# Chunkwise retention with its matmuls placed between the feed-forward matmuls

## The chip, the cores and the metric

The kernel runs on one core of a Trainium2 chip. The metric is the time of one execution in microseconds (us), measured on the device; a profile of one execution is taken beside it. All runs quoted here were in the fast state (no execution was over 1.5% above the fastest of its kernel), and each was compared with runs of the kernel before on the same chip.

In both kernels TensorE does the matrix products and leaves them in tiles of PSUM (called banks here); VectorE and ScalarE work on tiles element by element; GpSimd and SyncE mostly issue transfers (DMA) from and to the main memory, HBM (125 loads by GpSimd and 36 stores by SyncE on the page before). Before each matmul, TensorE loads one operand into its array (the weight load, PEld in the profiles; 2272 loads and 2272 matmuls on the page after).

## The reference

Causal retention over 8 batches, 8 heads, 576 positions and 64 dimensions, followed by a feed-forward layer with a quick Gelu. Cut to what matters:

```python
scores = (1 / np.sqrt(64)) * np.matmul(q, k.transpose(0, 1, 3, 2))   # q, k, v: (8, 8, 576, 64) fp32
gamma  = 1.0 - 2.0 ** (-5.0 - np.arange(8))
Dmat   = np.where(rel >= 0, gamma[:, None, None] ** rel, 0.0)        # rel = query position - key position
x      = np.matmul(scores * Dmat, v)     # then laid out as (4608 tokens, 512)
h      = x @ w_in                        # (512, 2048)
g      = h / (1.0 + np.exp(-1.702 * h))
out    = g @ w_out                       # (2048, 512), fp32
```

Because the decay is a power of gamma, `gamma ** (i - j)` splits into a factor of the query position and one of the key position. So the sum over old keys can be kept as a running 64 x 64 state per head instead of being computed again for every query.

## The kernel before

Two blocks, one after the other. The attention block works on one batch and two heads at a time (32 groups), with the full lower triangle of 576 x 576 scores. Three engines hand tiles to each other: TensorE makes scores, VectorE and ScalarE scale them, TensorE multiplies by v.

```python
# attention block, TensorE
T(0); T(1); A_w1(0)                 # T: transposes of q and k; A: scores; Bph: times v
for g in range(NG):                 # NG = 32
    if g >= 1: Bph(g - 1)
    A_w2(g)
    if g + 2 < NG: T(g + 2)
    if g + 1 < NG: A_w1(g + 1)
Bph(NG - 1)
...
# feed-forward block, TensorE: 4 matmuls up and 4 down for each of 9 chunks x 16 slices
hT(0); hT(1); hT(2)
for F in range(TOT):
    outmm(F)
    if F + 3 < TOT: hT(F + 3)
...
# feed-forward block: ScalarE makes the sigmoid, VectorE multiplies it in
act.activation(s_sb[F % 2].ap(), psH[F % 3].ap(), AF.Sigmoid, scale=1.702)
dve.tensor_tensor(gT[F % 4].ap(), psH[F % 3].ap(), s_sb[F % 2].ap(), ALU.mult)
...
# at each chunk end, ScalarE empties four banks over three staging tiles
for r in range(4):
    m = 4 * c + r
    if m >= 3:
        act.wait_ge(sem_ODMA[m % 3].sem, 16 * ((m - 3) // 3 + 1))
    act.activation(osb[m % 3].ap(), psOut[r].ap(), AF.Copy)
```

## Time and profile before

| | before |
|---|---|
| measured time | 439.0 us (median of 3) |
| attention block | to 165.6 us |
| feed-forward block, first to last matmul | 165.6 to 432.7 us, 267.1 us |
| 1152 feed-forward matmuls at their pitch of 216 ns | 248.8 us |

A word on pitch. A matmul line of the profile gives a duration, 380 ns for 512 columns, but in the timeline eight 512-column matmuls take 1.73 us, 216 ns each: one starts before the one before it has ended. So what a matmul costs here is the distance from its start to the next start.

The head of the page of the kernel before (busy time of each engine; then tenths of busy time in 40 slices of the span, and the granted TensorE clock in tenths; the lines of PEld, POOL and DMA are left out):

```profile
PE 363.5 (83%) x2600; PEld 177.9 (41%) x2624; DVE 219.3 (50%) x515; ACT 215.7 (49%) x390; POOL 105.5 (24%) x132
PE   0450588888888879998989989989989899899894
DVE  7660288888888883333433433433333343344331
ACT  3760388888888853334343343343433433433433
PEclk9995599999999997999999999999999999999999
```

Slices 1 to 15 are attention. From the sixth on, all three engines stand at 8 tenths nearly throughout, and none at 9: no engine is the limit by itself, they wait for each other. The fourth slice is empty. The table of windows of the same kernel (columns: stretch, its length, busy us and instructions of each engine, granted clock, DMA share, GB/s):

```profile
33.00:44.00 11.00, 0.00 (x0) 0.00 (x0) 0.00 (x0) 0.00 (x0) 2.45 (x3) 0.50 1.78 182
45.00:100.00 55.00, 43.76 (x598) 26.42 (x598) 41.47 (x123) 40.65 (x76) 54.54 (x66) 0.91 3.26 146
200.00:300.00 100.00, 94.26 (x422) 41.98 (x432) 37.35 (x54) 39.06 (x68) 0.00 (x0) 1.00 0.11 39
```

From 33 to 44 us nothing computes: the loads of the second batch stand behind 8 MB of weights (issued from 14.9 us on, the batch's from 18.3; w_out took 23.5 us to land, and TensorE began again at 49.3). From 200 us on, TensorE is busy 94 of 100 us. The missing part is at the chunk ends, as the timeline of one of them shows (start, duration, engine, line, what; in brackets the idle time before it and what ended it; the lines between these three are left out):

```profile
197.60 1.58 ACT L516 ACTIVATE osb<-psOut 128x512 f32<-128x512 f32 x3 [0.27 <-PE psOut L550]
200.33 0.60 ACT L516 ACTIVATE osb<-psOut 128x512 f32<-128x512 f32 x1 [1.16 <-DMA out_dram<-osb]
200.98 0.10 PEld L550 LDWEIGHTS psOut<-w_out_sb,gT 128*128 128x128 bf16 x1 [1.66 <-ACT osb L516]
```

The fourth copy waits 1.16 us for a store to free one of the three staging tiles, and TensorE's next weight load waits for that copy.

One more loss stands at the start of the block: in the window from 166 to 171 us the granted clock is 0.50, and the first 13 feed-forward matmuls start 0.43 us apart, twice 0.216, which costs about 2.7 us.

### The profile page before, as it was taken

What the parts mean: (1) busy time and instruction counts of PE and PEld (TensorE: products, weight loads), DVE (VectorE), ACT (ScalarE), POOL (GpSimd) and SP (SyncE); (2) the same over time, 40 slices, a digit from 0 to 9 for tenths busy, and PEclk for the clock granted to TensorE, in tenths of its full rate; (3) what the DMA queues carried; (4) which work ended last, traced back from release to release, by engine and by line L of the source; (5) the groups of instructions that cost most, each with busy time, mean ns of one, the idle gap of its engine ahead of it and who ended that gap; (6) DMA issues with size and microseconds to landing.
All of it is one profiled execution on the core that took longest, in us unless ns stands there. A gap on an engine that the chain in (4) does not pass through costs nothing.

```text
span 438.9 us, 7043 instructions
## 1 busy us (share of the span) xinstructions
PE 363.5 (83%) x2600; PEld 177.9 (41%) x2624; DVE 219.3 (50%) x515; ACT 215.7 (49%) x390; POOL 105.5 (24%) x132
## 2 busy tenths in 40 slices
PE   0450588888888879998989989989989899899894
PEld 0230355545554543443434434434444344344341
DVE  7660288888888883333433433433333343344331
ACT  3760388888888853334343343343433433433433
POOL 9972899997820000000000000000000000000000
PEclk9995599999999997999999999999999999999999
DMA  9999999999980000002011020020020200200202
GB/s 82 145 206 182 148 146 145 146 146 146 141 58 1 1 1 1 1 0 97 0 58 39 0 96 1 1 98 0 16 81 0 96 1 0 97 1 0 98 0 96
DMA packets 120369, 28.24 MB, mean 64 GB/s; under 512 B 113168, under 2 KB 115216, under 8 KB 120336
## 3 DMA queue, kind: packets, MB, share of 16 engines
q0 software_dynamic: 115152, 18.36, 72.2%
q1 hardware_dynamic: 5184, 9.44, 5.7%
q8 instruction: 21, 0.34, 0.4%
q14 instruction: 12, 0.10, 0.1%
HBM read 36.70 MB, written 9.44 MB: 105 GB/s over the span
## 4 chain that ended last, share of the span: by engine, by line
PE 55%; DMA 4%; ACT 2%; issue 1%
PE psOut L550 27%; PE psH L537 27%; DMA out_dram<-osb 4%; ACT osb L516 2%
## 5 line engine op out<-in xcount | busy, mean ns | idle before, releaser
L586 DVE TENSOR_TENSOR gT<-psH,s_sb 128x512 bf16<-128x512 f32 x144 | 99.6, 692 | 167.6 <-ACT s_sb L572 167.6
L550 PE MATMUL psOut<-w_out_sb,gT 128*128 128x512 bf16 x564 | 150.4, 380 | 12.1 <-ACT osb L516 10.5
L572 ACT ACTIVATE s_sb<-psH 128x512 bf16<-128x512 f32 x144 | 85.9, 597 | 151.4 <-PE psH L537 151.4
L537 PE MATMUL psH<-xT,w_in_sb 128*128 128x512 bf16 x564 | 148.2, 384 | 2.3 <-PEq L127 1.7
L550 PEld LDWEIGHTS psOut<-w_out_sb,gT 128*128 128x128 bf16 x576 | 56.5, 98 | 86.4 <-ACT osb L516 18.6
L537 PEld LDWEIGHTS psH<-xT,w_in_sb 128*128 128x128 bf16 x576 | 56.9, 99 | 69.7 <-issue 2.7
L426 ACT ACTIVATE rett_0<-psS_1,vfac 128x448 bf16<-128x448 f32 x64 | 37.1, 580 | 23.7 <-PE psS_1 L313 21.0
L253 PE MATMUL psTq<-ident,st_q 128*128 128x128 bf16 (+1 forms) x160 | 18.1, 228 | 35.7 <-issue 19.9
L459 DVE TENSOR_TENSOR rett_0<-psS_0,Emb 128x512 bf16<-128x512 f32 x32 | 22.1, 692 | 39.8 <-issue 36.4
L170 POOL DMA_DIRECT2D st_v<-in_v_dram x40 | 34.9, 1000 | 13.4 <-issue 10.8
L426 ACT ACTIVATE rett_1<-psS_1,vfac 128x448 bf16<-128x448 f32 x64 | 36.7, 573 | 0.0
L154 POOL DMA_DIRECT2D st_q<-in_q_dram x40 | 34.6, 975 | 3.5 <-issue 2.0
L161 POOL DMA_DIRECT2D st_k<-in_k_dram x40 | 34.7, 1006 | 0.0
L396 ACT ACTIVATE qT_sb<-psTq 128x576 bf16<-128x576 bf16 x32 | 20.8, 649 | 20.7 <-PE psTq L253 20.7
L253 PEld LDWEIGHTS psTq<-ident,st_q 128*128 128x128 bf16 (+1 forms) x160 | 10.8, 101 | 46.3 <-issue 43.5
L276 PE MATMUL psS_0<-qT_sb,kT_sb 64*128 64x128 bf16 x256 | 19.5, 226 | 10.2 <-DVE rett_0 L492 8.8
L340 PE MATMUL psO<-rett_0,st_v 128*64 128x512 bf16 (+3 forms) x128 | 27.7, 315 | 0.2 <-issue 0.2
L340 PE MATMUL psO<-rett_1,st_v 128*64 128x512 bf16 (+3 forms) x128 | 27.6, 315 | 0.1
L305 PE MATMUL psS_0<-qT_sb,kT_sb 64*64 64x64 bf16 (+2 forms) x192 | 20.0, 219 | 9.0 <-DVE rett_1 L459 8.6
L516 ACT ACTIVATE osb<-psOut 128x512 f32<-128x512 f32 x36 | 19.5, 598 | 14.1 <-DMA out_dram<-osb 9.9
L347 PE MATMUL psO<-rett_0,st_v 128*64 128x64 bf16 (+1 forms) x160 | 25.1, 199 | 0.0
L347 PE MATMUL psO<-rett_1,st_v 128*64 128x64 bf16 (+1 forms) x160 | 24.8, 199 | 0.0
(42 smaller groups left out, 301.4 us busy)
## 6 DMA issues: line engine op xcount, KB each, us to landing
out_dram<-osb SPq DMA_DIRECT2D x36, 256.0 KB, 2.3
st_q<-in_q_dram POOLq DMA_DIRECT2D x32, 128.0 KB, 9.2
st_k<-in_k_dram POOLq DMA_DIRECT2D x32, 128.0 KB, 9.2
st_v<-in_v_dram POOLq DMA_DIRECT2D x32, 128.0 KB, 9.1
w_in_sb<-in_moe_w_in_dram POOLq DMA_DIRECT2D x4, 512.0 KB, 10.7
w_out_sb<-in_moe_w_out_dram POOLq DMA_DIRECT2D x1, 2048.0 KB, 23.5
st_q<-in_q_dram POOLq DMA_DIRECT2D x8, 64.0 KB, 9.7
st_k<-in_k_dram POOLq DMA_DIRECT2D x8, 64.0 KB, 9.6
```

Source lines behind the costliest of these rows:

```text
L154: gp.dma_start(stq[0:rows, j, :, :], qkv_src(q, b, j)).then_inc(sem_q_[sl].sem, 16)
L161: gp.dma_start(stk[0:rows, j, :, :], qkv_src(k, b, j)).then_inc(sem_k_[sl].sem, 16)
L170: gp.dma_start(stv[0:rows, j, :, :], qkv_src(v, b, j)).then_inc(sem_v_[sl].sem, 16)
L253: pe.matmul(outT, lhsT, ident[0:rows, 0:rows], is_transpose=True).then_inc(sem_T.sem, 1)
L340: pe.matmul(o, lhsT, rhs, start=(j == 0), stop=(j == 3), skip_group_check=True,)
L347: mm = pe.matmul(o1, lhsT, rhs1, start=(j == 0), stop=(j == 4), skip_group_check=True,)
L426: act.activation(rett[rb][hh][:, jj, 128 : 128 + shi], psS[hh][1][:, 0:shi], AF.Copy, scale=vfac[:, NJ * head + jj : NJ * head + jj + 1],) ...
L516: act.activation(osb[m % 3].ap(), psOut[r].ap(), AF.Copy).then_inc(sem_OEV.sem, 1)
L537: mm = pe.matmul(psH[t].ap(), lhsT, rhs, start=(cc == 0), stop=(cc == 3))
L550: mm = pe.matmul(psOut[r].ap(), lhsT, rhs, start=(f == 0), stop=(f == NF - 1))
L572: act.activation(s_sb[F % 2].ap(), psH[F % 3].ap(), AF.Sigmoid, scale=1.702).then_inc(sem_sig.sem, 1)
L586: dve.tensor_tensor(gT[F % 4].ap(), psH[F % 3].ap(), s_sb[F % 2].ap(), ALU.mult).then_inc(sem_G.sem, 1)
```

## The change

Three things at once. Attention is done in 36 units of 128 tokens, all eight heads, with the state of old keys accumulating in a PSUM bank. Every matmul of a unit is 128 columns wide or less. And there is one instruction stream: each iteration issues one unit's attention matmuls and then 16 up-projection and 16 down-projection matmuls of earlier chunks (units run 4 ahead of the up-projection and 12 ahead of the down-projection). The quick Gelu is one ScalarE function (597 ns a tile on the page after, as the sigmoid before); VectorE no longer takes part in the feed-forward. A small recorder computes the semaphore waits from what each operation reads and writes.

The diff, cut to the main loop and the operations of a unit (setup, semaphores and the recorder are left out):

```diff
-NJ = 5
-JROWS = [128, 128, 128, 128, 64]
+NU = (B * S) // P          # 36 units
+LAG = 12
...
+        def state(u):       # running state: keys times values, accumulated in psK
+            for hp in range(HP):
+                op("pe", lambda e, hp=hp: e.matmul(
+                    psK[:, hp, :], kn[sl][:, 2 * hp : 2 * hp + 2, :],
+                    vp[u % 3][:, 2 * hp : 2 * hp + 2, :],
+                    start=(c == 0 and hp == 0), stop=True, skip_group_check=True), ...)
...
+        for t in range(-2, NU + LAG):
+            if t + 2 < NU:
+                scale_v(t + 2)                 # VectorE
+            if 0 <= t < NU:
+                state(t)                       # 4 matmuls
+            if t + 2 < NU:
+                transposes(t + 2)              # 8 matmuls, 1 VectorE copy
+            if 0 <= t < NU:
+                state_out(t)                   # VectorE
+                inter(t)                       # 4 matmuls, query times state
+                if t < 4:
+                    load_wout(t)
+                load(t + NLD)
+            if 0 <= t + 1 < NU:
+                scores(t + 1)                  # 8 matmuls on 64-row halves
+                scores_out(t + 1)              # 2 on VectorE
+            if 0 <= t < NU:
+                values(t)                      # 8 matmuls on 64-column halves
+                values_out(t)                  # VectorE
+            ch, hq = divmod(t - 4, 4)
+            co, r = divmod(t - LAG, 4)
...
+            for s in range(4):
+                if 0 <= ch < NCH:
+                    up(ch, 4 * hq + s, nh)     # 4 matmuls, 1 Gelu on ScalarE
+                    nh += 1
+                if 0 <= co < NCH:
+                    down(co, r, s, bank)       # 4 matmuls
+            if 0 <= co < NCH:
+                down_out(co, r, bank)          # 1 copy on ScalarE, 1 store
```

The load queue starts with the first four units, then w_in quarters alternating with units:

```diff
+        load_qk(0)
+        setup()
+        load_v(0)
+        for u in range(1, 4):
+            load(u)
+        for i in range(4):
+            load_win(i)
+            load(4 + i)
```

## The prediction

> **What bounds the kernel now.** It runs two phases in sequence. The table of windows shows TensorE at 19.4 of 20 us in the 180-200 us stretch and 94-95 of 100 us after it: the feed-forward phase (about 165.6 to 434 us) is bound by TensorE. Its steady pace in the timeline is 1.73 us for 8 matmuls of 512 columns, so 216 ns each. 1152 of them need 248.8 us; the phase takes about 268 us because at each of the 9 chunk ends the four output banks are emptied over three staging tiles, and the chain of waits has ScalarE waiting for an output store (up to 1.2 us) and TensorE waiting for ScalarE (up to 1.7 us).
> The first 165 us are attention. There every engine is partly idle: TensorE 43.8 of 55 us "busy" at 45-100 us, but those durations overlap. The timeline shows a 3.85 us period per head pair, a ping-pong of TensorE, VectorE and ScalarE; and no TensorE work at all from 33 to 44 us, where the second batch's loads queue behind 8 MB of weights.
>
> **What changes.** Attention becomes 36 units of 128 tokens, all heads, with a running state, and its matmuls stand between feed-forward matmuls. Attention no longer has its own 165 us; it costs only its TensorE time.
> - TensorE per unit, from start-to-start pitches in the before trace: transposes 8 x 56 ns; state 4 x 56; state times query 4 x 56; scores 8, two at a time on 64-row halves, 56 ns a pair; values 8, two at a time on column halves, 59 ns a pair. Sum 1.36 us. The trace shows 0.07-0.1 us lost at each change between full and half array; three or four changes give about 1.7 us per unit (estimate).
> - VectorE per unit: six tiles of 0.65-0.7 us (128x512 from PSUM: 692 ns before), about 4.2 us; the feed-forward multiply (692 ns x 144) disappears into one ScalarE Gelu. ScalarE per unit: four Gelus and one copy, 5 x 0.60 = 3 us. One full iteration is 32 x 216 ns + 1.7 = 8.6 us, so both are slack; in the 8 iterations without second matmuls it is 5.2 us, still above VectorE's 4.2.
> - DMA: same 36.7 MB read, but in the order needed. [...]
>
> **Sum.** Feed-forward can start when units 0-3 are done and, since TensorE is in order, unit 6's keys and queries have landed. With the before kernel's landed bytes over time (0.9, 2.5, 4.8 MB after 11, 22, 33 us) that is about 31 us. Then 31.5 + 248.8 + 31 units x 1.7 (53) [...] + 1 DMA stalls + 3.3 tail (one copy 0.6, one store about 2) = 340 us.
>
> Predicted 340 us, 8 in 10 within 330-356. Faster by over 2%: 0.98; within 2%: 0.01; slower: 0.01.
>
> **What would show it.** TensorE above 95% busy from about 35 us on; first up-matmul near 31 us; the chain of waits nearly all TensorE; 32 feed-forward matmuls plus attention in 8.6 us in the middle; VectorE about 50%, no ScalarE wait at chunk ends; DMA spread over 300 us.
>
> **What would make it wrong.** The start: units' loads delayed behind input weights (first up-matmul at 40 us). Small matmuls interleaved costing more than their pitch, because weight loads or semaphore waits break the pipeline (2.5 us per unit would add 25 us). VectorE setting the pace in the 8 iterations without second matmuls. Gelu slower than the sigmoid, with two PSUM banks instead of three.

Cut from the text: an allowance for a slow TensorE clock at the start of the feed-forward matmuls, with its term in the sum. The sum on record came to 339.3 us, put as 340; without the cut term of 1.7 us, the terms printed above come to 337.6.

## The result, and the profile after

The changed kernel took 338.58 us (median of 4 runs, 338.12 to 339.27) against 439.31 us. The ratio is 0.7703, with a 95% interval of 0.7676 to 0.7731. Ratios here are the mean time of one kernel's fast runs over that of the other's in the same rounds, so not quite the ratio of the medians quoted beside them. In the batches with the experiments the changed kernel itself, run again, took 339.33 us (0.7699).

The head of the page after, the same lines as before (the clock line is discussed below):

```profile
PE 316.9 (94%) x2272; PEld 162.5 (48%) x2272; DVE 132.6 (39%) x229; ACT 115.4 (34%) x198; POOL 108.5 (32%) x135
PE   1676999999999999999999999999999999999995
DVE  2687766864444434444444434444443200000000
ACT  5400345443333333333333333333333344442211
PEclk9999999999999999999999999999999999999999
```

From the fifth slice on, which begins at 33.7 us, TensorE is at 9 (90% or more) until the last slice. The table of windows says it in us:

```profile
45.00:100.00 55.00, 55.00 (x456) 28.97 (x455) 31.97 (x53) 23.28 (x39) 27.31 (x34) 1.00 1.34 159
100.00:200.00 100.00, 100.00 (x742) 51.90 (x740) 42.91 (x70) 34.63 (x58) 33.12 (x39) 1.00 0.69 95
```

One unit's attention in the middle of the run, TensorE alone, from the timeline (the values, eight lines from 151.43 to 151.63, are left out):

```profile
150.12 0.39 PE L305 MATMUL psK<-vp,kn 128*128 128x128 bf16 x4
150.34 0.39 PE L293 MATMUL psT<-ident,kn 128*128 128x128 bf16 x4
150.56 0.39 PE L293 MATMUL psT<-ident,qn 128*128 128x128 bf16 x4
150.79 0.39 PE L326 MATMUL psO<-qkT,kv_0 128*128 128x128 bf16 x4
151.10 0.40 PE L342 MATMUL psS<-qkT 64*128 64x128 bf16 x8
...
151.78 1.04 PE L374 MATMUL psH<-xT,w_in_sb 128*128 128x512 bf16 x4
```

Four full-array matmuls stand 0.22 us apart, 56 ns each. The eight scores, in pairs on row halves, take no longer than four full ones (0.40 us from the first start to the last end, against 0.39). No line has a bracket: nothing waited. The unit takes 1.66 us; the next unit starts at 158.70, an iteration of 8.58 us.

Adding up TensorE's starts over the whole trace gives the account of the span:

| part of the span | estimated in the prediction | measured, us |
|---|---|---|
| before the first feed-forward matmul | 31.5 | 33.8 |
| feed-forward matmuls, with the half-clock loss at their start | 248.8, and the cut 1.7 | 250.5 |
| attention after that point | 53 | 48.1 |
| waiting for loads after that point | 1 | 0 |
| from the last matmul's start to the end | 3.3 | 4.3 |
| sum | 339.3 | 336.7 |

The half-clock loss is visible in TensorE's weight loads at the start of the feed-forward, but not in the clock figure of the view. First the window, with a granted clock of 1.00 (the figure after the x5), then the loads in it from the timeline:

```profile
33.00:36.00 3.00, 3.00 (x21) 1.30 (x18) 3.00 (x6) 0.28 (x1) 3.00 (x5) 1.00 1.86 208
```

```profile
34.20 0.15 PEld L374 LDWEIGHTS psH<-xT,w_in_sb 128*128 128x128 bf16 x1 [0.28 <-issue]
34.63 0.15 PEld L374 LDWEIGHTS psH<-xT,w_in_sb 128*128 128x128 bf16 x1 [0.28 <-issue]
35.06 0.15 PEld L374 LDWEIGHTS psH<-xT,w_in_sb 128*128 128x128 bf16 x1 [0.28 <-issue]
```

They stand 0.43 us apart, twice the 0.216 of the matmuls later on; four matmuls were that slow, which cost 0.85 us.

The 1.00 is not a record of full clock. The clock events kept in this trace begin at 35.54 us, with full clock, and the view counts time without an event as full (so does the PEclk line above). From 35.48 us on the loads stand 0.22 us apart, so the event and the pitch agree. Where an event covers the slow stretch, the view does say 0.50: from 166 to 171 us in the kernel before, and from 150.8 to 153.1 us in the run `seq` below, whose first feed-forward loads also stand 0.43 us apart.

That the second row of the table matches to the tenth, with the cut term, is luck. The term allowed 1.7 us for a slow clock; 0.85 us was the clock, and another 0.85 us is one wait at 303.9 us, where a matmul starts 1.07 instead of 0.22 us after the one before because its bank has not been copied out.

The measured time of that execution is 338.57 us, 1.9 us more than the span. The prediction took its sum for the measured time, so part of its closeness is errors that cancel.

### The profile page after: what moved, and what is told of

Same layout as the page of the kernel before. It is cut to its first block, busy times and chain, and to the rows that moved or that the text cites. A ratio compares the mean times of both kernels' runs of the same rounds, so it can differ in the third digit from the quotient of the medians.

```text
span 336.7 us, 5221 instructions
## 1 busy us (share of the span) xinstructions
PE 316.9 (94%) x2272; PEld 162.5 (48%) x2272; DVE 132.6 (39%) x229; ACT 115.4 (34%) x198; POOL 108.5 (32%) x135
## 2 busy tenths in 40 slices
DMA packets 87447, 32.85 MB, mean 98 GB/s; under 512 B 76416, under 2 KB 80512, under 8 KB 87424
## 4 chain that ended last, share of the span: by engine, by line
PE 89%; POOL 6%; DMA 3%; ACT 0%; issue 0%; POOLq 0%
PE psH L374 38%; PE psY L392 31%; PE psS L392 4%; PE psT L293 4%; PE psO L359 3%; DMA qn<-in_q_dram 3%; PE psS L342 3%; PE psO L392 2%; POOL kn L200 2%; PE psK L305 2%; POOL vn L214 2%; POOL qn L200 2%; PE psO L326 1%; POOL w_in_sb L223 1%; ACT osb L401 0%; PE psO L332 0%
## 5 line engine op out<-in xcount | busy, mean ns | idle before, releaser
L379 ACT ACTIVATE gT<-psH 128x512 bf16<-128x512 f32 x144 | 86.0, 597 | 182.9 <-PE psH L374 182.9
L392 PE MATMUL psY<-w_out_sb,gT 128*128 128x512 bf16 x480 | 122.2, 379 | 0.7 <-ACT osb L401 0.7
L392 PEld LDWEIGHTS psY<-w_out_sb,gT 128*128 128x128 bf16 x480 | 46.5, 98 | 57.9 <-ACT osb L401 2.4
L296 DVE COPY qkT<-psT 128x1024 bf16<-128x1024 bf16 x36 | 24.8, 690 | 108.0 <-PE psT L293 107.9
L200 POOL DMA_DIRECT2D kn<-in_k_dram x40 | 36.8, 928 | 94.8 <-PE psK L305 80.3
L214 POOL DMA_DIRECT2D vn<-in_v_dram x40 | 37.4, 947 | 2.5 <-issue 2.4
L200 POOL DMA_DIRECT2D qn<-in_q_dram x40 | 37.0, 935 | 0.0
L284 DVE TENSOR_TENSOR vp<-vn,vfac 128x512 bf16<-128x512 f32 x36 | 24.6, 685 | 13.9 <-DMA vn<-in_v_dram 13.9
L350 DVE TENSOR_TENSOR pm_1<-psS,mask 128x512 bf16<-128x512 f32 x32 | 21.8, 680 | 0.0
L350 DVE TENSOR_TENSOR pm_0<-psS,mask 128x512 bf16<-128x512 f32 x32 | 21.8, 680 | 0.0
L359 PE MATMUL psO<-pm_1,vp 128*64 128x128 bf16 x144 | 15.9, 237 | 0.0
L359 PE MATMUL psO<-pm_0,vp 128*64 128x128 bf16 x144 | 15.9, 237 | 0.0
```

Source lines behind the costliest of these rows:

```text
L200: e.dma_start(dst[p0 : p0 + n, :, :], src[b, :, s0 : s0 + n, :].rearrange("h p d -> p h d"),)
L214: e.dma_start(vn[sl][p0 : p0 + n, :, :], v[b, :, s0 : s0 + n, :].rearrange("h p d -> p h d"),)
L284: op("dve", lambda e: e.tensor_tensor(vp[u % 3].ap(), vn[sl].ap(), vfac[:, ty, :, None].to_broadcast([P, H, DH]), ALU.mult), reads=[f"vn{s ...
L296: op("dve", lambda e: e.tensor_copy(qkT[u % 3].ap(), psT.ap()), reads=["psT"], writes=[f"qkT{u % 3}"])
L350: op("dve", lambda e, hh=hh: e.tensor_tensor(pm[u % 2][hh].ap(), psS[hh].ap(), m[:, None, :].to_broadcast([P, HP, P]), ALU.mult), reads=[f ...
L359: op("pe", lambda e, hp=hp, hh=hh: e.matmul(psO[64 * hh : 64 * hh + 64, hp, :], vp[u % 3][:, 2 * hp + hh, :], pm[u % 2][hh][:, hp, :], sta ...
```

## The experiments

Twelve runs were made, one of them the changed kernel again. All gave correct results.

### The yardstick: the changed kernel again

> The changed kernel unaltered, as the yardstick for the runs beside it on the same chip: 338 to 339 us.

339.33 us, ratio 0.7699. The first feed-forward matmul was at 34.0 us here.

### Is it the overlap, or the smaller work? The same units without interleaving

```diff
-        for t in range(-2, NU + LAG):
+        for t in range(-2, NU):
...
                 values(t)
                 values_out(t)
+        for t in range(4, NU + LAG):
             ch, hq = divmod(t - 4, 4)
```

Nine xT tiles (they hold attention's result, the input of the feed-forward) take the place of three, so that all attention can be finished first. The matmuls are the same.

> The changed kernel with the same units and the same matmuls, but no interleaving: all attention units first, then all feed-forward matmuls (nine xT tiles instead of three). Theory (the gain is the overlap; attention alone is bound by loads, VectorE and the chain between engines, not by TensorE): attention phase 36 units x 4.3 to 4.9 us = 155 to 180 us, then 249 us, so 410 to 430 us. Rival (the gain is the smaller work of the chunkwise form, interleaved or not): attention phase of 36 x 1.66 = 60 us plus a start of 10 to 20, total 325 to 345 us.

It took 407.54 us (407.32 to 408.41), ratio 0.9275. The first feed-forward matmul was at 150.8 us. The windows of this kernel show who was busy in the two parts:

```profile
45.00:100.00 55.00, 43.41 (x448) 31.09 (x446) 50.76 (x85) 0.00 (x0) 44.98 (x55) 1.00 1.80 199
200.00:300.00 100.00, 100.00 (x466) 44.07 (x464) 0.00 (x0) 43.43 (x74) 0.00 (x0) 1.00 0.11 40
```

and the chain of waits between 59 and 63 us says what set the pace (start, duration, what):

```profile
59.45 1.20 DVE pm L350 x2
60.65 0.60 DVE xT L368
61.24 0.60 DVE vp L284
61.84 0.60 DVE qkT L296
62.44 0.60 DVE kv L315
63.04 1.20 DVE pm L350 x2
```

It is VectorE without a gap: six tiles of 0.60 us, 3.6 us per unit. That is the pace from 60 us on; before, units came 4.3 to 5.7 us apart from 21 us on, with VectorE and TensorE waiting for loads in between. The theory had said 4.3 to 4.9 us per unit and 410 to 430 us, so the mechanism (loads, then VectorE, not TensorE) holds and its size was too large. The rival (325 to 345 us) falls. Going to the chunkwise form, with the cleaner feed-forward part that comes with it, is worth 32 us of the gain (439.8 to 407.5); letting the two parts share the time is worth the other 68 (407.5 to 339.3; the two kernels ran in different batches, with 439.8 and 440.0 us for the kernel before). The split holds for this order of steps: the old attention was not run interleaved, and what the single Gelu function is worth was not isolated.

### Is TensorE really the limit, and is 56 ns the price? Every transpose twice

```diff
-                for hp in range(HP):
+                for hp in [h for h in range(HP) for _ in range(2)]:
                     op("pe", ... is_transpose=True ...)
```

> Every transpose is issued twice (same input, same place, result unchanged): 8 more matmuls of 128 columns per unit. Theory (TensorE is the only limit once feed-forward has started, and an interleaved small matmul costs its 56 ns pitch and nothing else): 8 x 56 ns = 0.45 us in each of the 30 units that are transposed after the start, so +13.4 us, 352 us. Rival 1 (TensorE has slack in the pipeline, another engine or DMA sets the pace): under +3 us. Rival 2 (interleaved small matmuls cost much more than their pitch): over +20 us.

351.82 us, 12.5 us more than the yardstick. In the trace a unit's attention went from 1.66 to 2.11 us, as its first line and the feed-forward's next show:

```profile
148.26 0.39 PE L305 MATMUL psK<-vp,kn 128*128 128x128 bf16 x4
...
150.37 1.04 PE L374 MATMUL psH<-xT,w_in_sb 128*128 128x512 bf16 x4
```

The difference is 8 x 56 ns; over the 29 units transposed after the start it is 13.0 us. So TensorE had no slack that could have hidden the extra matmuls, and a small matmul among large ones costs its pitch and nothing more. Both rivals fall.

### What does a change of array shape cost?

```diff
+            if 0 <= t + 1 < NU:
+                scores(t + 1, (0, 1))
             if 0 <= t < NU:
                 inter(t)
...
-                scores(t + 1)
+                scores(t + 1, (2, 3))
```

> The score matmuls of a unit (64-row halves) are split in two groups with the state-times-query matmuls (full array) between them; same matmuls, two more changes between full and half array in the 28 units that have a state. Theory (each change of array use costs about 0.1 us beyond the 0.056 us pitch: 0.15 us from start to start in the after trace): 28 x 2 x 0.1 = +5 to +6 us. Rival (the 0.1 us is a wait for a semaphore or VectorE that happens to stand there): 0 to +1 us.

343.99 us, 4.7 us more, just under the expected 5 to 6. A unit with a state took 1.88 us instead of 1.66, for two more changes: 0.11 us each. The expectation counted 28 units with a state; 24 of them stand after the first feed-forward matmul, and there the attention grew from 48.1 to 53.2 us. The timeline of such a unit, where the scores now stand on both sides of the state product:

```profile
153.29 0.39 PE L293 MATMUL psT<-ident,qn 128*128 128x128 bf16 x4
153.61 0.29 PE L342 MATMUL psS<-qkT 64*128 64x128 bf16 x4
153.83 0.40 PE L326 MATMUL psO<-qkT,kv 128*128 128x128 bf16 x4
154.16 0.29 PE L342 MATMUL psS<-qkT 64*128 64x128 bf16 x4
```

The first four transposes of q need 0.22 us, but the scores start 0.32 us after them. That is about 0.1 us lost at the change, and 0.11 us by the unit's total. The changed kernel has three such changes per unit, and about 0.1 us is lost at each in its timeline above: from full array to row halves (scores, 151.10), to column halves (values, 151.43) and back (151.78). What TensorE does in that time the traces do not show.

### Is VectorE slack?

Two more multiplies per unit, into scratch tiles:

```diff
+            for x in range(2):
+                n = (2 * u + x) % 4
+                op("dve", lambda e, n=n: e.tensor_tensor(
+                    junk[n].ap(), vn[sl].ap(),
+                    vfac[:, ty, :, None].to_broadcast([P, H, DH]), ALU.mult), ...)
```

> Two more VectorE multiplies of 128x512 per unit, 0.6 to 0.69 us each, into scratch tiles. Theory (VectorE is slack in the 8.58 us iterations, and close to the pace only in the eight 5.12 us iterations without second matmuls and in the start): VectorE per unit rises from about 4.2 to 5.4 us, +2 to +7 us, all of it before 76 us; middle iterations stay at 8.58 us. Rival (VectorE sets the pace): +1.2 us per unit, over +35 us.

339.61 us, 0.3 us more than the yardstick: slack, even more of it than expected. The windows of this kernel, first in the stretch of the short 5.12 us iterations, then in the middle:

```profile
45.00:74.00 29.00, 29.00 (x273) 15.34 (x271) 27.95 (x47) 13.30 (x23) 19.28 (x24) 1.00 1.88 215
100.00:200.00 100.00, 100.00 (x752) 52.35 (x751) 57.39 (x94) 34.87 (x60) 33.26 (x39) 1.00 0.69 95
```

VectorE is busy 27.95 of 29 us and TensorE still 29.00 of 29. The error in the expectation was to add up busy durations (0.68 us each). Back-to-back tiles start 0.60 us apart, so eight of them need 4.8 us and fit in 5.12. The +2 us lower bound was missed for that reason. Only the start was 1.0 us later (first feed-forward matmul at 35.0 us).

### How much of the gain could the feed-forward part have had alone?

The kernel before with six staging tiles:

```diff
-osb = [sb(f"osb{i}", [P, 512], FP32) for i in range(3)]
+osb = [sb(f"osb{i}", [P, 512], FP32) for i in range(6)]
-                        act.wait_ge(sem_ODMA[m % 3].sem, 16 * ((m - 3) // 3 + 1))
+                        act.wait_ge(sem_ODMA[m % 6].sem, 16 * ((m - 6) // 6 + 1))
```

(and the same modulus at the other places)

> The kernel before with six output staging tiles instead of three: takes away ScalarE's wait for an output store at the chunk ends, nothing else. Theory (of the about 19 us that the feed-forward phase lies above 1152 x 216 ns, the store wait of 1.2 us at each of 8 or 9 chunk ends is half): -8 to -10 us, 430 us. Rival (the store wait is hidden and the four ScalarE copies in a row are the whole stall): 0 to -2 us. Either way it says how little of the 100 us gain can be had in the feed-forward phase.

429.23 us, ratio 0.9764: 10.5 us less, as the theory had it. The feed-forward block shrank from 267.1 to 256.7 us. The timeline of the same chunk end (other lines are left out):

```profile
195.93 2.06 ACT L516 ACTIVATE osb<-psOut 128x512 f32<-128x512 f32 x4 [0.27 <-PE psOut L550]
197.07 0.10 PEld L550 LDWEIGHTS psOut<-w_out_sb,gT 128*128 128x128 bf16 x1 [0.33 <-ACT osb L516]
197.56 0.10 PEld L550 LDWEIGHTS psOut<-w_out_sb,gT 128*128 128x128 bf16 x1 [0.40 <-ACT osb L516]
198.05 0.10 PEld L550 LDWEIGHTS psOut<-w_out_sb,gT 128*128 128x128 bf16 x1 [0.39 <-ACT osb L516]
```

The four copies now follow each other, and TensorE follows the copies. The store wait was about 10 of the 18 us that the block lay above its floor of 248.8. Of the 7.9 us that are left, about 5.9 us are lost where the matmuls follow the four copies (in each of eight chunk ends three of them start 0.40 to 0.49 instead of 0.22 us apart), and about 1.8 us the half clock at the start of the block. The changed kernel empties one bank per iteration, beside other matmuls, and keeps one such wait of 0.85 us.

### The start: what does it wait for?

The first feed-forward matmul came at 33.8 us, not at 31. TensorE's timeline in the changed kernel's start (lines are left out at the dots, and the value lines before the last line):

```profile
21.50 0.61 PE L293 MATMUL psT<-ident,kn 128*128 128x128 bf16 x4 [1.09 <-DMA kn<-in_k_dram]
...
26.41 0.61 PE L293 MATMUL psT<-ident,kn 128*128 128x128 bf16 x4 [0.77 <-DMA kn<-in_k_dram]
...
31.32 0.61 PE L293 MATMUL psT<-ident,kn 128*128 128x128 bf16 x4 [0.77 <-DMA kn<-in_k_dram]
32.15 0.61 PE L293 MATMUL psT<-ident,qn 128*128 128x128 bf16 x4 [0.23 <-DMA qn<-in_q_dram]
32.69 0.61 PE L342 MATMUL psS<-qkT 64*128 64x128 bf16 x8
33.80 0.61 PE L374 MATMUL psH<-xT,w_in_sb 128*128 128x512 bf16 x1
```

One unit per 4.9 us, each time waiting for k. With each unit comes a quarter of w_in. TensorE took its work in the order of the program: unit 3's part of xT, the last that the first feed-forward matmul reads, was written by 31.67 us, but that matmul came at 33.80, behind unit 6's transposes, which waited for q until 32.15, and the matmuls after them. Two experiments asked what of that binds. First, bytes written: v was converted to bf16 on the way in, `FP32` to `BF16` in the `vn` tiles.

> v is converted to bf16 on its way in, as before, so each unit writes 384 KB instead of 512 KB; reads are unchanged. Theory (the start is bound by bytes read from HBM and by their order, not by bytes written): first up-matmul stays near 33.8 us, total within 1 us of the changed kernel. Rival (the start is bound by bytes written to SBUF): first up-matmul 2 to 4 us earlier, total 2 to 4 us less.

339.53 us, and the first feed-forward matmul at 33.96 us: no change. Bytes written don't bind. A unit and a quarter of w_in are 3 x 262,144 + 1,048,576 bytes to read, 1.84 MB in 4.9 us, about 374 GB/s (an estimate from the period above). The traces speak for bytes read. Between 20 and 30 us the run with v in bf16 sends 702 packets per us instead of 531 (packet: the piece in which the page counts what the DMA moves) and writes 181 GB/s instead of 212, yet reads 360 GB/s against 367 (an estimate from the packets' sizes; q, k and w_in are twice as large in HBM as on landing). So neither the number of packets nor the bytes written set the pace. A run that reads fewer bytes was not made, so the limit was not isolated. Second, the order of the queue:

```diff
-        for i in range(4):
-            load_win(i)
-            load(4 + i)
+        load_win(0)
+        for u in (4, 5, 6):
+            load(u)
+        load_win(1)
+        load(7)
...
-                if t < 4:
-                    load_wout(t)
+                if t < 2:
+                    load_win(2 + t)
+                elif t < 6:
+                    load_wout(t - 2)
```

> Only the order of the load queue changes: the second to fourth w_in quarters and the w_out quarters are issued after the units that TensorE needs before its first feed-forward matmul. Theory (TensorE is in order and waits for unit 6's query, which lands 11 us after issue behind 2.5 MB of w_in; two quarters fewer in front of it are about 4.5 to 6 us): first up-matmul near 28 us, total 332 to 335 us. Rival (the start is bound by the chain between VectorE and TensorE, or the delayed weights stall it later): within 1.5 us of the changed kernel.

334.53 us, ratio 0.7611: 4.8 us faster than the yardstick, from a change of order alone. The total was as expected, the first feed-forward matmul (30.8 us) was not: 28 had been expected. The profiled runs, 4.4 us apart, show where the rest came from: the start is 3.2 us shorter, and the feed-forward matmuls take 1.2 us less because full clock began with the first of them (its event is at 31.0 us), while the yardstick had six slow ones. Part of the total is thus the clock, which the theory did not name. In the same stretch of this kernel's timeline the later units no longer wait for a load but for VectorE:

```profile
24.70 0.61 PE L305 MATMUL psK<-vp,kn 128*128 128x128 bf16 x4 [0.66 <-DVE kv L315]
...
26.49 0.61 PE L326 MATMUL psO<-qkT,kv 128*128 128x128 bf16 x4 [0.33 <-DVE xT L368]
```

Its last two units before the feed-forward come 3.6 us apart, which is the VectorE pace of the run without interleaving. So the start has a second limit just below the first.

### Three attempts to shorten the start further

The first moves the transposes of unit t+2 into the feed-forward matmuls from t = 4 on:

```diff
             for s in range(4):
+                if s == 2 and t >= 4 and t + 2 < NU:
+                    scale_v(t + 2)
+                    transposes(t + 2)
```

> On top of the later weights (334.5 us, first up-matmul at 30.8 us), the v scaling and the transposes of unit t+2 are issued in the middle of iteration t's feed-forward matmuls from t = 4 on, so that the first feed-forward matmul waits for unit 5 and not for unit 6. Theory (in the start, VectorE's six tiles per unit now set the pace, 3.6 us per unit, and TensorE in order waits behind them): first up-matmul 1.5 to 2.5 us earlier, about 29 us; total 332 to 333.5 us; iterations stay at 8.58 us. Rival (transposes between feed-forward matmuls cost a new wait, because the copy of the transposed tile comes too late for the scores): total above 335 us.

A miss: 337.57 us, 3 us slower than the kernel that it starts from. The theory had the start earlier by 1.5 to 2.5 us; it came at 31.5 us. The rival fails as well, in its reason: a unit's attention still took 1.22 + 0.45 us, and an iteration did not grow. The profile shows where the time went (the values are left out):

```profile
30.29 0.61 PE L342 MATMUL psS<-qkT 64*128 64x128 bf16 x7 [0.31 <-DVE pm L350]
31.46 3.60 PE L374 MATMUL psH<-xT,w_in_sb 128*128 128x512 bf16 x8
34.84 0.63 PE L293 MATMUL psT<-ident,kn 128*128 128x128 bf16 x4
```

TensorE, freed of the transposes, waits for VectorE instead, so it gained nothing. And the eight feed-forward matmuls that follow take from 31.46 to 34.84 us, 0.42 us each: half clock (the trace's first clock event, full clock, is at 36.2 us). In the kernel that it starts from, one matmul of the first 16 was that slow. That is a cost of about 2 us which neither theory had named. Why the clock rose later here was not tested; the number of slow matmuls varied between 0 and 10 over the profiled runs, also among kernels with the same start (full clock from 35.5, 36.6 and 38.2 us in the changed kernel, in its repetition and in the run with v in bf16), and each run has one profile.

The second moves the copies of units 2 to 5 to ScalarE, idle at that time:

```diff
+            if 2 <= u < 6:
+                op("act", lambda e: e.activation(qkT[u % 3].ap(), psT.ap(), AF.Copy), ...)
```

> In addition the copies of the transposed tile of units 2 to 5 go from VectorE to ScalarE, which has nothing to do between 12 and 30 us. Theory (VectorE's serial tiles set the start's pace): up to 4 x 0.6 us less, first up-matmul at 27 us, total 330 to 331.5 us. Rival (the loads set it again as soon as VectorE is relieved): under 1 us less than the run beside it.

336.08 us, 1.5 us better than the run beside it, but the intervals of the two ratios overlap (0.7619 to 0.7674 and 0.7650 to 0.7692). The first feed-forward matmul came at 30.5 instead of 31.5 us, where 27 had been expected, and full clock began at 32.6 instead of 36.2 us. The earlier start agrees with VectorE as the pace, but less was gained than the 2.4 us of work moved, and the total stayed above the expected 330 to 331.5. How much of the 1.5 us is the clock is open.

The third loads v through SyncE's queue, so that GpSimd has less to issue:

> In addition v, which needs no conversion, is loaded through the SyncE queue instead of GpSimd's, so GpSimd spends 1.8 instead of 2.7 us per unit on issuing. Theory (by now the start is bound by issuing and landing of k and q): first up-matmul 1 to 3 us earlier than in the run beside it. Rival (the bytes themselves bind, or the output stores behind the v loads on the same queue come late): no gain, or a loss later.

346.79 us, 10.7 us worse. The first feed-forward matmul fell back to 36.5 us, and TensorE waited for k and q, there and again between 59 and 68 us. In the list of DMA issues the median time from issue to landing of k rose from 4.9 to 8.2 us, that of a w_in quarter from 9.9 to 26.1 us: eleven v loads were issued in the first 20 us and ran beside k, q and the weights. The second queue brought no more bytes per us. It brought fewer: between 10 and 30 us the DMA moved 167 GB/s instead of 198. Two things changed at once. The order of need that the single queue had kept was lost; and v was cut into 36,864 packets of 256 bytes, where GpSimd's queue had sent 2,304 of 4,096 (the page counts 122,008 packets in all instead of 87,447). Which of the two costs more was not tested.

Last, the later weights with the ScalarE copies, and the transposes back in their place:

> Later weights as in the 334.5 us run, transposes back in their old place, and the copies of units 2 to 5 on ScalarE. Theory (VectorE's serial tiles set the start's pace once the weights are out of the way; moving the transposes into the feed-forward was what cost, by half-clock matmuls at its start): first up-matmul at 29 to 30 us, the first 16 feed-forward matmuls in 3.5 to 3.8 us, total 332.5 to 334 us, ratio to before 0.757 to 0.760. Rival (ScalarE's slower copy, 1.02 us against 0.68, eats what VectorE gains, or the loads bind): ratio 0.760 to 0.763.

333.43 us (332.79 to 334.72), ratio 0.760, interval 0.7573 to 0.7626. The first feed-forward weight load came at 29.6 us (this trace lacks the record of its matmul), and the first iteration's 16 matmuls were through at 33.1 us, none of them slow, as the theory had it (full clock from 29.3 us). That agrees with the moved transposes having been what cost, but since the clock's rise also moves between runs with the same start, it does not show it. The total fits both the theory's range and the rival's lower end, and its interval overlaps that of the later weights alone (0.7599 to 0.7623), so its advantage over that kernel stays open. Both beat the changed kernel.

## Why the prediction was right

- "Feed-forward is bound by TensorE at 216 ns a matmul": right. The feed-forward matmuls took 250.5 us in the changed kernel, half-clock loss and one wait for a copy included.
- "Attention no longer has its own 165 us; it costs only its TensorE time": right, and the doubled transposes show it: 12.5 us more for 13.0 us of added pitch. The run without interleaving shows that this, and not the smaller work alone, is most of the gain.
- "About 1.7 us per unit": measured 1.66 us for a full unit. The sum took 1.7 for all 31; units without a state product or without a state update cost 1.44 us, and the last two have no transposes, so the average was 1.55 us and the total 48.1 instead of 53 us. The allowance for changes of the array was right in kind and size (0.11 us each).
- "First up-matmul near 31 us": 33.8, the largest miss in the sum after attention's. TensorE's wait for unit 6's query ended at 32.15 us instead of 31, and the matmuls from there to the first feed-forward matmul took 1.65 us where the sum had 0.5. The landing time had been taken from the bytes landed over time in the kernel before; in the changed kernel a unit and a w_in quarter came every 4.9 us. The later weights, which brought the first up-matmul to 30.8 us, show that this was the named risk "loads delayed behind input weights", in a small size.
- The cut term, 1.7 us for a slow clock at the start of the feed-forward: it was the author's estimate from a figure that no trace here shows. Measured were 0.85 us in this profile, from four matmuls at half clock, and between nothing and about 2 us in the others. In the trace of the kernel before, the granted clock was 0.50 from 31.0 to 54.9 us; TensorE stood idle for 19.9 us until 49.3 us, and full clock came 5.6 us after that.
- "VectorE about 4.2 us per unit, about 50% busy": its tiles start 0.60 us apart, so it needs 3.6 us; it was busy 39% of the span. The conclusion, slack, held.
- "No ScalarE wait at chunk ends": nearly. The weight loads waited 2.4 us in five places for a copy; one of them held up the matmuls, by 0.85 us, the others were hidden by matmuls in flight. Gelu took 597 ns, as the sigmoid before, and two banks were enough.
- "DMA spread over 300 us": not so for the loads. The last one was issued before 215 us; only stores follow.
- The total of 340 us (339.3 as summed, the cut term included) against 338.6 came from terms that erred in both directions: +4.9 us in attention and +1 for load stalls, -2.3 at the start, -1.0 at the tail, and -1.9 for the difference between span and measured time; the feed-forward row came out even with the cut term.

## What to carry to other kernels

When two phases are bound by different engines, try to issue them as one stream: here the cost of the one that isn't bound by TensorE fell to its matmul pitch (48.1 us of TensorE's time), which could be read from start-to-start times of the old trace before a line was written. Check the slack of the other engines with pitches as well, not with busy durations. Then look at the start: TensorE took its work in order, so what was loaded in front of the unit that it waited for (unit 6's q, until 32.15 us) delayed everything after it (the first feed-forward matmul, to 33.8), and reordering the queue was a cheap gain (4.8 us here, 3.2 of them in the start itself). And a clock figure of 1.00 before a trace's first clock event is no evidence; the distance between starts is (0.43 us before the event at 35.54 us, 0.22 after it).
